# A new order table for a two-branch sequence kernel: positions, buffer slots and copy engines changed, the same operations

## The chip, the cores and the metric

One core of a Trainium2 chip. The metric is the device time of one launch in microseconds (us). Before the change three runs gave 343.4, 344.65 and 345.7 us, the median being 344.65.

## The reference, cut to what matters

Two independent branches over a sequence of 2048 positions with 1024 channels, all bf16; their outputs stand side by side in the last axis.

```python
# branch A: short convolution of k (4 taps), times v, long convolution by FFT, times q
kv = k_shift * v
y  = irfft(rfft(kv, 4096) * rfft(ssm_k, 4096))[:2048] + kv * ssm_D
a  = q * y
# branch B: diagonal complex recurrence between two dense complex products
Bu = einsum("bld,pd->blp", x, B_bar)
h  = Lam_bar * h + Bu[:, t]              # over t
b  = 2 * einsum("blp,dp->bld", hseq, Cmat).real + x * Dskip
```

## The kernel before, in words

Nothing in this kernel is scheduled by a tool at run time. The text table ORDER holds 1489 words, one for each task, and the loop at L773 to L783 takes them in turn and issues the instructions of each. Every engine runs its own instructions in the order in which they were issued; between engines only semaphores wait. So the table fixes the order on each engine, and only that. A word such as `ue.14.3:a2` has the task, its indices, and the slots it takes: `a` a unit of an SBUF area of 53 units (2 KB a partition each), `p` one of 8 PSUM banks, `h` one of 3 state buffers, `w` one of 3 slots for Fourier matrices. A task that takes a slot waits for the last reader of what lay there. A `v` behind the name of a copy (`uev`, `skev`, `a3ev` ...) puts that PSUM copy on DVE instead of ACT.

Branch B works in 16 chunks of 128 positions. On PE, `U.i.jp.jl` (L464, 16 matmuls of 128x128) is the input product; `ue` (L473) copies it out of PSUM. On DVE, `r1` (L487) and `r2` (L498) rotate, two `sc` (L504) are the scan, `r3` (L487) and `r4` (L510) rotate back, all 16 chunks one after the other; a one-column copy `cy.i` on ACT (L500) hands the state from `r4.i-1` to the scan `sc.i`. The output product is `y` (L520, L523) or, in quarters of the array, `yq` (L538, 20 matmuls a task); `ye` (L556) copies it out, and `yst`, `ysg` (from POOL's queue), `ysp`, `ysh` (from SP's) store it.

Branch A is an FFT in stages. DVE forms kv in `kvm`, `kva`, `kvb`, `kvc` (L588 to L603); PE does the first stage in `am` (L608) for kv and in `hT` (L632) and `hm` (L657) for the filter; `ae` (L614), `hc` (L637) and `he` (L665) copy out, and stores to DRAM regroup the rows. For 16 pairs of frequency groups `sh` and `sk` (L688) make the second stage, `she` (L697) and `ske` (L704) copy out, a DMA (`sw` on POOL's queue, `swp` on SP's, L708) swaps real and imaginary rows, `pr` on DVE (L714) multiplies, `sa` on PE (L726) goes back, `sae` (L734) copies, `vst` stores. The last stage loads with `vl`, multiplies in `a3` (L754), copies in `a3e` (L761), multiplies with q in `qm` (L763) and stores with `ost` or `osp`.

At the start ACT also copies out the transposed B matrices (`bc`, L431, 16 of them, of which DVE does two as `bcv`, L427 and L429) and makes the rotation tables: `sin1`, `sin2` (L325, L332), `eo` (L348, L349), `z1`, `z2` (L357 to L362); DVE finishes a table in `stt` (L354, L355).

The loop that issues everything, and the one dependency that it adds by hand:

```python
for word in ORDER.split():
    task, _, slots = word.partition(":")
    ...
    E[f](*args)
```

Of the kernel before, what the change touches and what calls it, by code (L numbers as in the profile page):

```python
# [72 lines left out]
bT.2.1:p0 U.0.0.1 bT.3.0:p7 bc.5.0 bc.2.1 bc.5.1 kva.3 kring U.1.2.0:p5 bl.3.1:a23 cl.0.0:a14 bT.2.0:p2 bT.3.1:p0
bl.7.1:a46 ue.1.0:a34 U.0.2.1:p6 bc.3.1 bc.2.0 U.0.2.0 U.1.2.1 cl.3.0:a37 bl.7.0:a26 cl.1.0:a25 bT.7.1:p2 kvb.3:a22
bT.7.0:p0 ue.0.0:a23 bc.6.1 kp.-2 x.3:a21 U.0.1.0:p3 bc.3.0 gz stt cl.2.0:a12 cT.0.0:p4 bc.7.0 bc.7.1 U.0.1.1 U.0.3.0:p0
kvm.1:a15 ue.1.2 vp.1:a27 U.0.3.1 U.3.2.0:p1 ue.0.1 U.3.0.0:p3 z1 kvm.2:a42 z2 ld_Q U.1.1.1:p2 ue.0.2 ue.0.3 x.2:a52
U.1.1.0 cl.3.1:a13 kva.1 cT.1.0:p7 cl.2.1:a32 kva.2 kvb.1:a14 kvb.2:a39 ue.1.1 kvm.0:a15 rta kvc.3 U.3.0.1 cx.6.0 kva.0
# [10 lines left out]
he.0.7.0.0:a50 y.0.0.3 hc.0.0:a13 hm.0.6.0:p4p2 ye.0.0:a19 hm.0.4.1:p5p7 y.0.1.0:p6 y.0.1.1 y.0.1.2 y.0.1.3 vp.2:a34
kvb.4:a31 he.0.6.0.0 sc.1.1 he.0.4.1.1 vp.3:a26 r1.2:a14 he.0.4.1.0 he.0.7.0.1 hst.0.7.0 r3.1:a46 hm.0.0.1:p1p5
hst.0.4.1 hc.0.5:a42 he.0.6.0.1 r4.1 hm.0.0.0:p2p3 he.0.0.1.0:a48 cy.2:h1 r2.2 hm.0.5.1:p7p0 ye.0.1 he.0.5.1.1:a23  # L90
he.0.5.1.0 kp.3 he.0.0.1.1 kvm.6:a38 he.0.0.0.0 y.1.1.0:p4 kvc.4 y.1.1.1 hst.0.6.0 hst.0.6.1 kp.4 kva.6 hst.0.5.1
hm.0.5.0:p6p0 he.0.5.0.0 kvm.5:a14 y.1.1.2 he.0.0.0.1 kvb.6:a25 he.0.5.0.1 y.1.1.3 hm.0.7.1:p2p7 ye.1.1:a28 he.0.7.1.0
kva.5 am.4.0:p1p6 y.1.0.0:p4 he.0.7.1.1 x.4:a32 hm.0.3.0:p2p3 ae.4.0.0:a29 hm.0.3.1:p5p0 hst.0.0.1 hst.0.0.0
he.0.3.1.0:a36 kvc.6 y.1.0.1 he.0.3.1.1 hst.0.5.0 kvb.5:a12 sc.2.1 ae.4.1.0 he.0.3.0.1 kvm.7:a13 y.1.0.2 am.4.1:p1p7
hl.3.0:a40 he.0.3.0.0 hm.0.1.0:p5p0 y.1.0.3 he.0.1.0.0:a38 am.6.1:p5p6 ae.4.1.1 U.4.3.1:p7 he.0.1.0.1 ae.6.0.1:a17
hl.2.1:a44 U.4.3.0 kvc.5 ae.6.1.1 am.6.0:p6p5 U.4.0.0:p2 ae.4.0.1 ue.4.3:a23 U.4.1.1:p3 ae.6.0.0 hm.0.2.0:p0p6 ae.6.1.0
ye.1.0 kva.7 hm.0.1.1:p5p7 sc.2.0 hm.0.2.1:p1p4 hst.0.7.1 hl.3.1 he.0.2.0.0:a34 U.4.1.0 he.0.1.1.0 hl.2.0 he.0.2.1.1
# [5 lines left out]
y.2.0.2 kvm.8:a48 r4.3 y.2.0.3 he.1.7.1.0 ae.7.0.1 hc.1.2:a31 y.2.1.3 ye.2.0:a47 hm.1.4.1:p4p6 ae.7.1.1 kva.8
hm.1.7.0:p3p5 ye.2.1 yq.3.0:p1p0 hst.0.1.1 he.1.7.0.1 he.1.7.0.0 hm.1.4.0:p7p2 yst.2 he.1.4.1.0:a29 kvm.9:a39 lw.3:w1
kvb.8:a38 he.1.4.0.1 vp.4:a12 yq.3.1 yq.3.2 he.1.4.1.1 he.1.4.0.0 hm.1.3.0:p5p6 he.1.3.0.1:a15 hm.1.3.1:p3p4 he.1.3.1.0
hst.1.7.0 he.1.3.1.1 yq.3.3 hm.1.2.1:p7p6 x.6:a37 he.1.2.1.0:a19 kva.9 he.1.2.1.1 he.1.3.0.0 kvc.8 x.5:a36 lw.1:w2
kvb.9:a35 kvm.10:a47 U.6.1.0:p3 U.6.1.1 am.8.1:p6p7 ast.7 hst.1.7.1 r1.4:a40 kva.10 ae.8.1.1:a44 hst.1.4.1 ae.8.0.1
r2.4:h0 am.8.0:p5p2 ae.8.0.0 ae.8.1.0 hst.1.4.0 ue.6.1:a38 yq.3.4 yq.3.5 hm.1.2.0:p5p7 he.1.2.0.0 x.7:a27 kp.7
hm.1.5.1:p2p6 he.1.5.1.1:a51 he.1.5.1.0 hst.1.5.1 yq.3.6 yq.3.7 ye.3.1:a24 hm.1.5.0:p6p4 kvm.11:a28 he.1.2.0.1 hst.1.2.0
hm.1.0.1:p3p5 cy.4 he.1.5.0.0 kp.6 kvb.10:a33 U.5.1.1:p2 U.5.1.0 sc.4.0 U.6.3.0:p7 kva.11 sc.4.1 hst.1.3.1 ye.3.0  # L110
ue.5.1:a40 he.1.0.1.0:a17 U.5.3.1:p2 hm.1.0.0:p3p1 kvc.9 ast.8 he.1.5.0.1 hst.1.5.0 kvb.11:a46 hm.1.6.0:p0p6 he.1.0.0.0
he.1.0.0.1 he.1.6.0.1:a47 U.5.3.0 hst.1.2.1 hst.1.3.0 U.6.3.1 he.1.6.0.0 U.6.0.1:p1 hm.1.1.0:p6p0 ue.5.3 ysp.3
hm.1.1.1:p2p3 he.1.0.1.1 hm.1.6.1:p5p4 he.1.1.0.0:a22 U.6.0.0 r3.4:a42 he.1.6.1.0 kvm.13:a12 he.1.1.1.1 U.5.2.0:p6
ue.6.0 U.5.2.1 he.1.6.1.1 hst.1.6.1 r4.4 he.1.1.1.0 hst.1.1.1 U.7.0.0:p3 he.1.1.0.1 vp.5:a50 U.5.0.0:p0 hst.1.0.1
hst.1.0.0 kvc.10 am.9.0:p2p4 kvc.11 kva.13 U.7.0.1 ae.9.1.0:a29 kvm.15:a49 ae.9.0.0 ue.7.0:a24 U.5.0.1 U.7.3.0:p4 ue.5.0
am.9.1:p1p0 vp.7:a34 ae.9.0.1 x.10:a26 kvb.13:a17 U.7.3.1 vp.6:a42 am.10.0:p3p1 kvm.14:a18 kvm.12:a13 kva.15 yq.4.0:p5p2
yq.4.1 yq.4.2 yq.4.3 ae.10.0.0:a44 ae.10.1.0 ue.7.3 ae.9.1.1 am.11.1:p3p0 ue.5.2 U.7.1.0:p1 kvc.13 ue.6.3 am.10.1:p4p6
# [725 lines left out]
```

## Time and profile before

| | us |
|---|---|
| span of the profiled execution | 343.2 |
| median of three runs | 344.65 |
| busy: PE, DVE, ACT, POOL | 329.5, 325.1, 273.5, 68.9 |
| TensorE clock granted, mean | 0.996 of full speed |
| DMA | 100.83 MB in 62592 packets |

The profile was taken of one execution; its span, from the first instruction to the last, is 343.2 us, and the only time around it is that of the runs: 343.4 us for the lowest, 344.65 us in the median. Three engines are busy nearly throughout: PE 96% of the span, DVE 95%, ACT 80%. The share of a matmul group in the busy time counts matmuls that wait inside PE's pipeline; the distance from one start to the next is what a matmul costs when PE is not held up. The chain that ended last runs mostly through PE.

### The profile page before, as it was taken

The page shows a single profiled execution, that of the slowest core. Times are in us where ns is not written, and L with a number is a line of the kernel's source. Part 1 is how long each engine was busy: PE and PEld are TensorE (multiplying, and loading weights), DVE is VectorE, ACT ScalarE, POOL GpSimd, SP SyncE. Part 2 cuts the span into 40 slices and gives each one's busy share as a digit, 9 for nine tenths or more (in the row PEclk, how much of TensorE's full clock was granted, in tenths as well). Part 3 has the DMA queues.
Part 4 walks back from the last instruction along what each step waited for, and adds up shares of the span by engine and source line. Part 5 has one row for each costly group of instructions (what it writes and reads, how often), then busy time and mean ns, then how long its engine had stood idle before and what let it go on. Part 6 is the DMA issues. An engine that isn't in the chain of part 4 may idle for free.

```text
span 343.2 us, 11813 instructions
## 1 busy us (share of the span) xinstructions
PE 329.5 (96%) x5086; PEld 230.2 (67%) x5105; DVE 325.1 (95%) x263; ACT 273.5 (80%) x519; POOL 68.9 (20%) x111
## 2 busy tenths in 40 slices
...
GB/s 177 352 351 208 315 281 283 155 318 365 368 269 198 264 263 295 233 261 343 313 353 282 270 339 212 369 272 311 280 314 276 216 326 378 327 335 284 375 346 274
DMA packets 62592, 100.83 MB, mean 294 GB/s; under 512 B 29422, under 2 KB 31614, under 8 KB 62540
## 3 DMA queue, kind: packets, MB, share of 16 engines
...
## 4 chain that ended last, share of the span: by engine, by line
PE 74%; ACT 15%; DMA 4%; issue 3%; DVE 3%; SPq 0%; POOL 0%; DVEq 0%; POOLq 0%
PE bank L464 25%; PE bank L538 19%; PE bank L520 10%; PE bank L754 4%; PE bank L688 4%; PE bank L726 4%; PE bank L608 2%; PE bank L657 2%; ACT BT L431 2%; ACT arena L614 2%; ACT arena L473 2%; ACT CT L439 2%; ACT arena L637 2%; DMA wslot<-a_c_W 1%; DMA arena<-arena 1%
## 5 line engine op out<-in xcount | busy, mean ns | idle before, releaser
L464 PEld LDWEIGHTS <-BT 128*128 128x128 bf16 x2048 | 117.8, 98 | 14.4 <-issue 9.9
L464 PE MATMUL bank<-arena,BT 128*128 128x128 bf16 x2048 | 125.4, 221 | 1.1 <-ACT BT L431 0.9
L538 PE MATMUL bank<-CT,gslot 64*64 64x512 bf16 x1408 | 86.6, 378 | 0.0
L504 DVE TENSOR_TENSOR_SCAN gslot<-rtab,gslot 128x1040 bf16<-128x1040 f32 x32 | 73.0, 2311 | 0.5
L538 PEld LDWEIGHTS <-gslot 64*64 64x64 bf16 x1408 | 36.9, 107 | 30.8 <-issue 1.9
L473 ACT CAST arena<-bank 128x512 bf16<-128x512 f32 x63 | 40.5, 660 | 13.8 <-PE bank L464 13.4
L614 ACT CAST arena<-bank 128x512 bf16<-128x512 f32 x64 | 37.2, 680 | 6.7 <-PE bank L608 4.0
L697 ACT CAST arena<-bank 128x512 bf16<-128x512 f32 x63 | 35.0, 617 | 5.9 <-issue 2.8
L520 PE MATMUL bank<-CT,gslot 128*128 128x512 bf16 x153 | 38.5, 380 | 0.3
L665 ACT CAST arena<-bank 128x512 bf16<-128x512 f32 x64 | 35.2, 631 | 3.1 <-PE bank L657 3.0
L714 DVE TENSOR_TENSOR arena<-arena 128x4096 bf16<-128x4096 bf16 x16 | 36.5, 2280 | 1.1 <-DMA arena<-arena 1.0
L487 DVE TENSOR_TENSOR arena<-gslot,Z 128x4096 bf16<-128x4096 bf16 x16 | 36.6, 2287 | 0.8 <-DVE gslot L504 0.2
L704 ACT CAST arena<-bank 128x512 bf16<-128x512 f32 x60 | 34.4, 621 | 3.2 <-PE bank L688 3.0
L734 ACT CAST arena<-bank 128x512 bf16<-128x512 f32 x60 | 32.4, 616 | 5.5 <-PE bank L726 5.3
L487 DVE TENSOR_TENSOR arena<-arena,Z 128x4096 bf16<-128x4096 bf16 x16 | 36.5, 2280 | 0.1
L556 ACT CAST arena<-bank 128x512 bf16<-128x512 f32 x31 | 18.1, 599 | 16.6 <-PE bank L538 8.7
L588 DVE TENSOR_TENSOR arena<-arena 128x4096 bf16<-128x4096 bf16 (+3 forms) x16 | 30.0, 1881 | 0.0
L668 POOL DMA_DIRECT2D Ys_h<-arena x32 | 23.2, 735 | 25.5 <-ACT arena L665 20.2
L617 POOL DMA_DIRECT2D Ys_kv<-arena x16 | 11.2, 726 | 83.5 <-ACT arena L614 81.1
L520 PEld LDWEIGHTS <-gslot 128*128 128x128 bf16 x160 | 14.1, 98 | 15.9 <-issue 2.3
L688 PE MATMUL bank<-arena,wslot 64*64 64x512 bf16 x256 | 21.5, 382 | 0.3 <-DMA wslot<-a_c_W 0.3
L737 POOL DMA_DIRECT2D Vs<-arena x16 | 11.7, 731 | 46.3 <-ACT arena L734 41.3
...
## 6 DMA issues: line engine op xcount, KB each, us to landing
Ys_kv<-arena POOLq DMA_DIRECT2D x16, 512.0 KB, 5.6
...
arena<-Ys_h SPq DMA_DIRECT2D x16, 512.0 KB, 5.0
arena<-Ys_kv SPq DMA_DIRECT2D x16, 512.0 KB, 5.6
Vs<-arena POOLq DMA_DIRECT2D x16, 512.0 KB, 5.6
arena<-Vs SPq DMA_DIRECT2D x16, 512.0 KB, 6.7
...
arena<-in_A_k_dram SPq DMA_DIRECT2D x8, 512.0 KB, 5.2
```

The costliest lines, as they stand in the source:

```text
L464: nc.tensor.matmul(pu[:, w, jl, :], BT[:, 2 * jp + jl, w, d, :], xT[:, d, :], start=(d == 0), stop=(d == ND - 1))
L473: cp(st["u", i][:, :, 2 * jp:2 * jp + 2, :], st.pop(("pu", i, jp)))
L487: nc.vector.tensor_mul(m, s_, win(Z))
L504: nc.vector.tensor_tensor_scan(gf, rtab[:].rearrange("p j t -> p (j t)"), gf, 0.0, ALU.mult, ALU.add)
L520: nc.tensor.matmul(py, h[:, w, j, 2:GW], CT[:, j, w, dh * 512:(dh + 1) * 512], start=(j == 0 and w == 0), stop=False)
L538: mm = nc.tensor.matmul(st["py", i, dh][cols, cs(r)], lhs(dh, rows, c), rhs(dh, rows), start=first, stop=last)
L614: cp(st["ysb", n2][:, p, dh * 512:(dh + 1) * 512], st.pop(("pa", n2, p, dh)))
L665: cp(o, st.pop(("pb", hf, s, e, r)).rearrange("p (n c t) -> p n c t", n=2, c=2))
L688: nc.tensor.matmul(st["ps", nm, g, l][64 * dh:64 * dh + 64, :], st["w", i][rows, a * WC:a * WC + 64], st[nm, i][rows, a, dh * 512:(dh + 1) ...
L697: cp(st["hab", i][:, 0, a, l, :], st.pop(("ps", "h", g, l)))
L704: cp(st["x16", i][:, a, l, :], st.pop(("ps", "k", g, l)))
L714: nc.vector.tensor_mul(hab, st.pop(("x16", i)).rearrange("p a l d -> p (a l d)").unsqueeze(1).to_broadcast([P, 2, 2 * D]), hab)
```

## The change

Only the table is new; every other line of the program is the same. It has 1489 words again, each task of before once. What differs:

- the position of most words, and the slots that they take;
- which engine copies out of PSUM: 22 copies on DVE before (2 of B matrices, 4 `skev`, 4 `saev`, 1 `shev`, 1 `uev`, 1 `yev`, 9 `a3ev`), 14 now (3 `uev`, 6 `yev`, 1 `skev`, 4 `a3ev`), so eight more are on ACT;
- which queue stores the output of branch B: three whole-chunk stores moved from SP (7 to 4) to POOL (7 to 10), and one half-chunk store from POOL to SP; the eight stores of branch A are 3 on SP and 5 on POOL where they were 4 and 4.

The core of the diff, the table's first and last rows:

```diff
 ORDER = """
-ld_w:a22 wb.3:p3 ld_par wbe.3:a8 par_T:p4 wb.0:p5 wb.7:p1 p32 ld_F bl.1.0:a39 bl.0.1:a18 wb.5:p7 bl.6.0:a34 bl.4.1:a14
-exp1 dve2 wbe.0 dve3 wb.6:p2 wb.4:p3 wb.2:p0 sm_pre wbe.7 bl.0.0:a27 wbe.5 x.0:a38 wb.1:p7 wbe.6 exp2 kp.1:a0 bl.1.1:a21
...
-y.15.1.3 ysg.14.1 ost.3 ye.15.1:a1 ysg.15.1 y.15.0.0:p4 y.15.0.1 a3e.15.0 y.15.0.2 qm.7 osp.7 y.15.0.3 ye.15.0 ysh.15.0
+ld_w:a13 ld_par par_T:p3 p32 bl.5.1:a27 dd bl.0.1:a17 bl.0.0:a39 exp1 kp.0:a0 wb.3:p2 dve2 bl.1.1:a40 bl.5.0:a42 kp.1
+wb.5:p4 wbe.3:a8 bl.1.0:a51 x.0:a52 dve3 tabA1:a44a28a35a37 sm_pre wb.4:p0 wb.7:p1 wbe.5 kp.-1 wbe.4 tabA2 wb.6:p6 wbe.7
...
+ysg.14.1 yev.15.0:a41 ost.0 ysh.15.0 ye.15.1 ysh.15.1
```

Three places show what this does to the engines.

DVE near the end of the frequency stage. L714 is `pr` (two of the rows are `pr.14` and `pr.13`), L487, L498, L504 and L510 are the steps of a chunk, and the number of a gslot tells the chunk's buffer. Before:

```order
L487 TENSOR_TENSOR arena_95<-gslot2_91,Z2_78 128x4096
L704 CAST arena_95<-bank6_102 128x512
L714 TENSOR_TENSOR arena_95<-arena_95 128x4096
L510 TENSOR_TENSOR gslot2_91<-arena_95 128x16x128
L714 TENSOR_TENSOR arena_95<-arena_95 128x4096
L734 CAST arena_95<-bank2_98 128x512
L487 TENSOR_TENSOR arena_95<-arena_95,Z1_77 128x4096
L498 TENSOR_TENSOR gslot0_89<-arena_95 128x16x128
```

Now:

```order
L487 TENSOR_TENSOR arena_95<-gslot2_91,Z2_78 128x4096
L510 TENSOR_TENSOR gslot2_91<-arena_95 128x16x128
L714 TENSOR_TENSOR arena_95<-arena_95 128x4096
L473 CAST arena_95<-bank5_101 128x2x256
L487 TENSOR_TENSOR arena_95<-arena_95,Z1_77 128x4096
L498 TENSOR_TENSOR gslot1_90<-arena_95 128x16x128
L704 CAST arena_95<-bank2_98 128x512
L714 TENSOR_TENSOR arena_95<-arena_95 128x4096 x2
```

The end of chunk 12 (L510) and the first two steps of chunk 13 (L487, L498) are now ahead of `pr.14`, which is the first of the two L714 in the last row (the L714 above it is `pr.12`); before, `pr.14` was the first L714 shown and all three stood behind it.

ACT around the hand-over of the state to chunk 3, `cy.3`, which is the L500 row in the middle. Before:

```order
L637 COPY arena_95<-bank5_101 128x1024
L637 COPY arena_95<-bank6_102 128x1024
L637 COPY arena_95<-bank4_100 128x1024
L614 CAST arena_95<-bank7_103 128x512
L500 COPY gslot2_91<-gslot1_90 128x16
L645 ACTIVATE arena_95<-arena_95,p32_118 128x1 x2
```

Now:

```order
L614 CAST arena_95<-bank4_100 128x512
L614 CAST arena_95<-bank1_97 128x512
L637 COPY arena_95<-bank7_103 128x1024
L473 CAST arena_95<-bank5_101 128x2x256
L500 COPY gslot0_89<-gslot1_90 128x16
L637 COPY arena_95<-bank3_99 128x1024
```

The copy just ahead of `cy.3` is now a `ue` (L473), which needs a `U` of PE; before it was an `ae` (L614).

ACT at the start, from `exp2` (L293) on. Before:

```order
L293 ACTIVATE r<-a__130 128x8
L314 ACT_TABLE_LOAD
L314 ACTIVATE so<-sv 128x16
L431 ACTIVATE BT<-bank_100 128x1024
L408 CAST arena<-bank_96 128x4x128
L408 CAST arena<-bank_103 128x4x128
L325 ACTIVATE arena<-arena,hpi 128x1024
L408 CAST arena<-bank_99 128x4x128
L431 ACTIVATE BT<-bank_102 128x1024
L332 ACTIVATE arena<-arena 128x1024
L431 ACTIVATE BT<-bank_97 128x1024
L348 ACTIVATE arena<-arena,b_224 128x128
```

Now, the rows just ahead of the same L348:

```order
L408 CAST arena<-bank_98 128x4x128
L314 ACT_TABLE_LOAD
L314 ACTIVATE so<-sv 128x16
L431 ACTIVATE BT<-bank_101 128x1024
L431 ACTIVATE BT<-bank_97 128x1024
L431 ACTIVATE BT<-bank_99 128x1024
L325 ACTIVATE arena<-arena,hpi 128x1024
L332 ACTIVATE arena<-arena 128x1024
L348 ACTIVATE arena<-arena,b_229 128x128
```

Six copies of B matrices (L431) are now ahead of the 16 instructions of `eo`, which begin with L348; before there were three.

More of the change, by code (lines that the diff above doesn't have):

```diff
@@ L73 @@
[L73 to L77, printed above, removed]
@@ L88 @@
[L88 to L92, printed above, removed]
@@ L93 @@
[L93 to L97, printed above, removed]
@@ L103 @@
[L103 to L107, printed above, removed]
@@ L108 @@
[L108 to L117, printed above, removed]
@@ new lines @@
+wbe.6 bT.0.1:p7 exp2 ld_Q bc.0.1 bT.5.1:p0 bc.5.1 bl.4.1:a41 wb.2:p2 wbe.2 bl.3.0:a27 bT.0.0:p7 bc.0.0 wb.0:p0 wb.1:p2
+wbe.0 wbe.1 kvm.3:a17 bT.5.0:p5 bT.1.0:p1 sin0 par_rest bT.1.1:p3 bc.5.0 ld_F bc.1.0 U.0.0.0:p2 x.1:a51 bl.6.1:a49
+bc.1.1 sin1 sin2 eo U.0.2.1:p3 U.0.0.1 ue.0.0:a47 kva.3 bT.6.1:p5 U.1.0.0:p6 bl.4.0:a39 bl.7.0:a30 bT.7.0:p1 bl.2.1:a16
+bc.7.0 bT.4.1:p4 bc.4.1 U.1.0.1 gz bT.4.0:p2 bc.4.0 bT.2.1:p1 kring kvm.1:a12 bl.7.1:a50 bc.2.1 bT.7.1:p4 bl.2.0:a22
+bc.7.1 bT.2.0:p0 bc.2.0 kvm.2:a23 kvb.3:a42 U.0.2.0 kp.-2 kva.2 kva.1 bl.6.0:a31 kvb.2:a39 lw.0:w0 bT.6.0:p7 bc.6.0
@@ new lines @@
+cl.2.0:a50 U.2.2.1:p2 U.2.2.0 ue.2.2 ast.2 cT.2.0:p7 cc.2.0 cT.2.1:p0 cc.2.1 sc.1.1 U.2.3.1 ue.2.3 hT.0.0:p2 hc.0.1:a31
+kva.4 hc.0.0:a19 hT.0.5:p5 hc.0.5:a26 hT.0.4:p7 hc.0.4:a32 y.0.0.0:p1 y.0.0.1 hT.0.7:p3 hc.0.7:a34 ld_G y.0.0.2
+hm.0.6.1:p6p2 he.0.6.1.1:a22 he.0.6.1.0 y.0.0.3 hst.0.6.1 hm.0.7.0:p5p4 he.0.7.0.0:a49 he.0.7.0.1 r3.1:a13 hst.0.7.0
+kvb.4:a24 hm.0.4.0:p3p7 he.0.4.0.1:a29 he.0.4.0.0 hm.0.4.1:p2p0 he.0.4.1.1 he.0.4.1.0 hst.0.4.1 cx.5.1 hst.0.4.0 r4.1
+kp.3 kvm.6:a41 ye.0.0:a17 cx.5.0 cx.7.0 cx.4.1 cx.7.1 cx.4.0 y.0.1.0:p6 y.0.1.1 y.0.1.2 hm.0.0.0:p3p7 he.0.0.0.0:a47
```

190 lines of the change are left out of this document (105 added, 85 removed).

## The prediction

> **What bounds the kernel now.** I read the busy times first, then the waits of DVE, then the chain that ended last, then the end of the program in the timeline.
>
> ```profile
> PE 329.5 (96%) x5086; PEld 230.2 (67%) x5105; DVE 325.1 (95%) x263; ACT 273.5 (80%) x519; POOL 68.9 (20%) x111
> PE 74%; ACT 15%; DMA 4%; issue 3%; DVE 3%; SPq 0%; POOL 0%; DVEq 0%; POOLq 0%
> ```
>
> Two engines look full, and the chain is PE's. The first row cannot tell which of the two is the bound; the waits say more.
>
> ```profile
> DVE p L284 <- PE bank L279: 3.5, 1, 3.5
> DVE arena L601 <- PE bank L415: 1.3, 1, 1.3
> DVE arena L714 <- DMA arena<-arena: 1.0, 2, 0.6
> ```
>
> DVE waits 3.5 us for the first parameters, and after that hardly ever: 1.3 us once at the start, 1.0 us in all for two swap DMAs, the rest less. So DVE runs on its own work from 4.48 us on. PE reads what DVE makes, and arrives just behind it:
>
> ```profile
> 279.11 2.28 DVE L714 TENSOR_TENSOR arena<-arena 128x4096 bf16<-128x4096 bf16 x1
> ...
> 281.31 1.49 PE L726 MATMUL bank<-arena,wslot 64*64 64x512 bf16 x24
> ...
> 222.09 2.28 DVE L714 TENSOR_TENSOR arena<-arena 128x4096 bf16<-128x4096 bf16 x1
> ...
> 224.43 1.06 PE L726 MATMUL bank<-arena,wslot 64*64 64x512 bf16 x16
> ```
>
> `pr.14` ends on DVE at 281.39 us. The three `sa` from 281.31 us are sa.24, sa.28 and sa.29; sa.28, the first reader of pr.14, is the second third of the row and starts about 0.4 us behind pr.14's end. `pr.6` ends at 224.37 us, and sa.12 starts 0.06 us later. Behind each such meeting PE has only its own work. So the time is **DVE's work up to a result, plus PE's work from that result's reader to the end, for the pair where this sum is largest**, plus waits and the tail:
>
> ```profile
> 336.05 1.03 PE L520 MATMUL bank<-CT,gslot 128*128 128x512 bf16 x4
> ...
> 336.97 1.03 PE L520 MATMUL bank<-CT,gslot 128*128 128x512 bf16 x4
> 337.83 0.22 PE L523 MATMUL bank<-Dd,arena 128*128 128x128 bf16 x1
> ...
> 335.52 1.23 DVE L763 TENSOR_TENSOR arena<-arena 128x2048 bf16<-128x2048 bf16 x1 [0.73 <-ACT arena L761]
> ...
> 302.11 1.07 ACT L556 CAST arena<-bank 128x512 bf16<-128x512 f32 x2 [4.63 <-PE bank L538]
> ...
> 338.70 0.34 SPq L560 DMA_DIRECT2D out_dram<-arena  x1
> ```
>
> PE ends at 338.05, 1.3 us after DVE's last instruction (336.75); a copy, a store of 128 KB issued at 338.70 and its landing fill the 5.15 us to 343.2.
>
> **The change, part by part.** What a task costs on PE is the distance between starts when PE runs on:
>
> ```profile
> 163.19 4.57 PE bank L464 x80
> 176.56 0.86 PE bank L726 x16
> 296.52 7.28 PE bank L538 x160
> 306.56 1.73 PE bank L754 x8
> ```
>
> A `U` (16 matmuls) is 0.90, an `sa` (8) 0.43, a `yq` (20) 0.90, an `a3` (2) 0.43, and a `y` 0.92 by the two L520 rows above. On DVE:
>
> ```profile
> 312.10 2.28 DVE L487 TENSOR_TENSOR arena<-arena,Z 128x4096 bf16<-128x4096 bf16 x1
> 314.30 1.28 DVE L761 CAST arena<-bank 128x512 bf16<-128x512 f32 x2
> 315.50 1.21 DVE L498 TENSOR_TENSOR gslot<-arena 128x2048 bf16<-128x2048 bf16 x1
> ...
> 308.44 1.22 DVE L510 TENSOR_TENSOR gslot<-arena 128x2048 bf16<-128x2048 bf16 x1
> 309.59 1.28 DVE L761 CAST arena<-bank 128x512 bf16<-128x512 f32 x2
> ```
>
> From start to start an `r1` is 2.20, a copy 0.60, an `r2` or `r4` 1.15.
>
> *The meeting of DVE and PE.* At pr.14 and sa.28, before: PE has 4 sa, 12 U, 16 yq, 32 a3 and 16 y left, 1.7 + 10.8 + 14.4 + 13.8 + 14.7 = 55.4 us, and from 281.77 that makes 337.2; it ends at 338.05, so 0.9 us are lost behind. Now DVE does one r1, one r2 and one r4 more ahead of pr.14 (+4.5) and six copies fewer (11 to 5, -3.6): +0.9. PE has three U fewer left and one sa more: -2.3. The sum at this pair falls by 1.4. I made the same count at every result of DVE that PE reads. Before, the largest sums lie together: pr.6 with sa.12, pr.14 with sa.28 (0.1 less) and r4.10 with yq.10.0 (0.2 less). At pr.6 DVE now has 2.3 less ahead (no r1.10 and no B copies, but r4.9: -2.20 - 1.20 + 1.15) and PE the same behind; at r4.10 DVE has 1.2 less (the two B copies, which are ACT's now) and PE the same. So r4.10 and pr.14 carry the end now, and the largest sum falls by **1.4 us**, not by all the eight copies. Bounds: 0, if a pair that I rate lower takes over through a wait of its own, and -2.3, by the pair that falls most.
>
> *The eight copies.* On DVE they were 8 x 0.60 = 4.8 us. Most of them leave behind the last meeting (nine `a3ev` become four), where PE no longer waits for DVE. On ACT they are free there: the L556 row above stands behind an ACT gap of 4.63 us, and ACT is busy 17.3 of the last 43 us.
>
> *The start.* The 1.3 us that DVE waited for PE at L601 (kvb.3, whose slot was that of a B matrix still being transposed) goes; kvb.3 takes other units and stands two kvm later. In its place r1.0 comes to wait for ue.0.1 on ACT:
>
> ```profile
> 27.76 3.81 ACT L431 ACTIVATE BT<-bank 128x1024 bf16<-128x1024 bf16 x4
> 31.38 1.15 ACT L473 CAST arena<-bank 128x512 bf16<-128x512 f32 x2
> 32.32 1.16 ACT L357 ACTIVATE Z<-Z 128x1024 bf16<-128x1024 bf16 x1
> ```
>
> A B copy is 0.90 from start to start, a 512-column copy 0.48. Ahead of ue.0.1 ACT has 16 B copies (14.4), 8 wbe and 5 ue (6.2), eo (4.7) and 3.5 of exp, sin and z1: 28.8, from 4.8 us with a table load of 1.3, so ue.0.1 ends near 35.6. DVE has 30.3 of work ahead of r1.0 and is there near 35.2: a wait of 0.4 for one of 1.3. Bounds 0 and -1.3; I take **-0.9**.
>
> *ACT in the first 100 us.* Here a wait is added.
>
> ```profile
> 14.73 0.44 ACT L348 ACTIVATE arena<-arena,b 128x128 f32<-128x128 f32 x1
> ...
> 19.41 1.92 ACT L431 ACTIVATE BT<-bank 128x1024 bf16<-128x1024 bf16 x2
> ...
> 35.16 1.13 ACT L362 ACTIVATE Z<-arena 128x1024 bf16<-128x1024 f32 x1
> ...
> 49.12 2.28 DVE L487 TENSOR_TENSOR arena<-gslot,Z 128x4096 bf16<-128x4096 bf16 x1
> ...
> 94.69 0.38 ACT L500 COPY gslot<-gslot 128x16 bf16<-128x16 bf16 x1
> ...
> 95.19 4.53 DVE L504 TENSOR_TENSOR_SCAN gslot<-rtab,gslot 128x1040 bf16<-128x1040 f32 x2
> ...
> 0.00:100.00 100.00, 93.15 (x1151) 73.21 (x1161) 92.93 (x111) 93.94 (x162) 22.63 (x41) 1.00 0.99 288
> ```
>
> The L500 row is cy.3; the scan behind it started 0.12 us after it ended, so it had no slack. Ahead of cy.3 ACT now has two B copies, one ue, one ae and two short adds more, 2 x 0.90 + 2 x 0.48 + 0.4 = 3.1 or 3.2 us; DVE has 1.0 more ahead of that scan. If ACT were always busy, DVE would wait 2.1 us. But ACT was busy 93.9 of the first 100 us, and the first 4 were its start, so some 2 us of pauses can take it up. Bounds 0 and +2.1; nearer to the lower, I take **+0.7**. Behind a late scan are r3.3 and every later step of DVE, and so PE.
>
> *Stores and loads.* Three stores of 256 KB go from SP's queue to POOL's. POOL is busy 20%, and its stores land as soon as SP's transfers (5.6 us for 512 KB on each):
>
> ```profile
> Ys_kv<-arena POOLq DMA_DIRECT2D x16, 512.0 KB, 5.6
> ...
> arena<-Ys_kv SPq DMA_DIRECT2D x16, 512.0 KB, 5.6
> ```
>
> Nothing of it is on the path: 0. The tail keeps its form, copy and 128 KB store on SP: 0; a 512 KB store on POOL's queue just ahead of it could add up to 1.
>
> The sum: -1.4 - 0.9 + 0.7 = **-1.6 us**, from a span of 343.2 to 341.6. The runs' median stands 1.45 above that span, so 344.65 becomes **343.0**.
>
> **The rivals.** *DVE is the bound.* If PE's place behind DVE were only an accident of the old order, all of DVE's saving would be time: 4.8 + 0.9, less the 0.7 at cy.3 = 5.0, 344.65 to **339.6**. For it: 95% busy and hardly a wait. Against it: DVE's last instruction ends 1.3 us ahead of PE's, and PE's last 55 us hold 0.9 us of waits. The Trainium skill, Perfetto Trace Analysis, section Identifying the Most-Contended Engine, has this rule: matmul busy time overstates how full PE is, and LDWEIGHTS busy should be used, with the engine of highest occupancy improved first. By that PE's 67% would leave DVE's 95% as the engine to relieve; the trace agrees that busy PE time is inflated (a matmul of L464 is shown for 221 ns and costs 0.90 us / 16 = 56), but PE's starts follow each other without a gap at the end, which goes against the rule here.
>
> ```profile
> L464 PE MATMUL bank<-arena,BT 128*128 128x128 bf16 x2048 | 125.4, 221 | 1.1 <-ACT BT L431 0.9
> ```
>
> *ACT becomes the bound of the first 100 us: slower.* `eo` (14.73 to 19.41 us before) starts behind six B copies instead of three, some 3 us later, and with it the ACT tasks that DVE waits for (z2, the last ue of chunks 3 and 1, cy.3). In the old order z2 ended at 36.29 and its reader r3.0 started at 49.12, 12.8 us later; now r3.0 has 3.4 us less of DVE's work ahead of it and z2 8.4 us more of ACT's, which leaves 1 us. Once ACT pauses for PE in that stretch by over 1 us in all, each further microsecond goes to DVE. Pauses as before, 2 to 3 us, with eo's 3.1 and cy.3's 2.1 give +5.2; with -1.4 and -0.9 that is +2.9: **347.5**. For it: 93.9 of 100 us busy, and more work there. Against it: ACT's pauses were waits for PE, and PE's order is now ahead of ACT's in this stretch, so they should shrink.
>
> *Slots at the last moment.* `x.1` on SP's queue now takes the slot of a B matrix and waits for its transpose (bT.1.0); eight B loads behind it on that queue wait too. Ahead of that transpose PE has 5.3 us of work, from 4.2 us on, and waits for some copies of ACT: x.1 goes out near 11.3 us, where it went out at 7.82:
>
> ```profile
> 7.82 1.74 SPq L447 DMA_TRANSPOSE arena<-in_B_x_dram  x1
> ```
>
> If its 3.5 us are not hidden behind ACT's eo, the U of chunk 1 and the last B copies come late and take back the 1.4 us: the old time, **344.6**.
>
> **How the numbers follow.** Forecast 0.50, DVE the bound 0.26, ACT the bound 0.17, late slots 0.07. A measurement here tells about 1% from no change, 3.4 us: faster is below 341.2, slower above 348.1. The forecast's own range is 340.7 to 345 by its bounds; a tenth of it lies below 341.2. Faster: 0.05 + most of the 0.26 = 0.29. Slower: under half of ACT's 0.17, which reaches 350, and a little for what I do not see: 0.13. Within 1%: 0.58. The range goes from 339.0, the middle of the DVE case and a little more, to 347.5.
>
> **What would show it.** Right: DVE's last instruction ends several us ahead of PE's; sa.28 still starts within 1 us of pr.14's end; no L601 wait at the start; PE's end near 336.5 with the same 5 us behind it. The ACT rival shows as DVE waiting on L500, L473 or L360 to L362 for 2 us or more before 100 us. The DVE rival shows as PE ending at 333 to 334. Wrong at the root would be a DVE wait of over 2 us on a DMA after 150 us.

## The result: slower by 1.4%, and the profile after

The changed kernel takes 349.16 us (median of six runs, 347.23 to 351.38) where the kernel before takes 345.42 (six runs). The two medians lie 3.7 us apart. The ratio on record is 1.0136, with a 95% interval of 1.0104 to 1.0169, which on 345 us is 4.7 us; below, this ratio is used, since every experiment has one like it. The forecast was 343.0, 1.6 us less than before. The profiled execution took 349.38, its span is 347.6. Two executions of the experiments, 354.65 and 360.73 us, ran slower at a granted clock of 0.986 and 0.978; the ratios leave them out, and the second of them is the one that was profiled for the reverse by slots.

First the busy times and DVE's waits after the change, to be held against the two shown of before:

```profile
PE 330.8 (95%) x5105; PEld 230.5 (66%) x5105; DVE 322.4 (93%) x255; ACT 277.8 (80%) x527; POOL 70.7 (20%) x114
...
DVE arena L763 <- ACT arena L761: 3.3, 3, 1.9
DVE p L284 <- PE bank L279: 3.1, 1, 3.1
DVE arena L714 <- ACT arena L704: 2.9, 3, 1.6
DVE gslot L504 <- ACT gslot L500: 2.6, 1, 2.6
DVE arena L487 <- ACT arena L473: 2.0, 3, 0.9
```

DVE has less work, as the change says, and yet arrives later. Before, its waits on ACT were one of 0.7 us and one of 0.4; now ten of the fifteen waits that the list of after has, 10.8 of their 16.2 us, are for ACT. Where that counts, the windows of DVE show: first of before, up to pr.14 and from there to the end, then of after, cut at the same place (columns: the stretch, its length and DVE's busy time, then granted clock, DMA share and GB/s).

```profile
4.50:279.10 274.60, 269.04 (x221) 1.00 0.97 289
279.10:343.20 64.10, 55.91 (x41) 0.98 0.93 331
```

```profile
4.50:285.80 281.30, 271.60 (x217) 1.00 0.94 287
```

pr.14 comes 6.7 us later: 2.6 us more of busy time and 4.1 more of waits (5.6 before, 9.7 now). Half of the additional busy time lies in one place, the eight instructions of `dd`, which the new table puts first and which take 1.25 us longer there, one row of after and one of before:

```profile
4.45 2.63 DVE L371 TENSOR_SCALAR Dd<-ident,p 128x128 bf16<-128x128 bf16 x8
```

```profile
11.84 1.38 DVE L371 TENSOR_SCALAR Dd<-ident,p 128x128 bf16<-128x128 bf16 x8
```

The delay builds up along the way: r1.0 starts 1.8 us earlier than before, sc.3.0 2.0 us later, pr.3 2.8 us later and pr.14 6.7. From pr.14 to the end it is 64.1 us before and 347.6 - 285.8 = 61.8 now, 2.3 less. The meeting itself still stands, in the timeline of after:

```profile
285.83 4.48 DVE L714 TENSOR_TENSOR arena<-arena 128x4096 bf16<-128x4096 bf16 x2
...
288.38 1.49 PE L726 MATMUL bank<-arena,wslot 64*64 64x512 bf16 x24
```

pr.14, the first of the two, ends at about 288.1, and sa.28 starts 0.3 us later. So the meeting held, and the whole loss lies ahead of pr.14.

ACT's waits show something that the kernel before has not. Of before, no row of ACT's waits names a DMA. Of after, three do:

```profile
ACT arena L614 <- DMA Ys_kv<-arena: 2.8, 2, 2.0
...
ACT arena L665 <- DMA Ys_h<-arena: 1.5, 1, 1.5
ACT arena L704 <- DMA Vs<-arena: 1.3, 1, 1.3
```

These are stores to DRAM. At three places ACT's copy waits until the store that still reads its slot has landed: ae.1.0.0 for ast.3 (1.96 us), he.0.3.0.1 for hst.0.6.0 (1.54) and ske.17.0 for vst.5 (1.35). Such a wait is called a hold from here on. The three are 4.8 us in all, of which 3.9 lie after the end of the copy's own matmul, so that no more than these are the store's alone. The rows add up to 5.6, which is the number in the expectations below, but the second wait of the first row, 0.83 us in front of ae.13.1.1, is no hold. By the table that copy writes units 28 and 29, while ast.11, the store that lands just then, reads 23 and 24; and the copy's own matmul, the last of the second row here, ended 0.04 us before the copy began:

```profile
147.43 0.58 ACT L614 CAST arena<-bank 128x512 bf16<-128x512 f32 x1 [0.83 <-DMA Ys_kv<-arena]
```

```profile
146.79 0.59 PE L608 MATMUL bank<-arena,F1t 128*128 128x512 bf16 x2
```

In the profile of the kernel with two places mended by order (below) the same 0.83 us stand in front of that copy, although ast.11 had landed 1.8 us earlier. So the table fixes more than the order on each engine: its slots decide which copy has to wait for which store. The timeline at the first of the three, ae.1.0.0:

```profile
47.69 0.84 ACT L614 CAST arena<-bank 128x512 bf16<-128x512 f32 x1
...
50.48 0.58 ACT L614 CAST arena<-bank 128x512 bf16<-128x512 f32 x1 [1.96 <-DMA Ys_kv<-arena]
50.96 0.59 ACT L473 CAST arena<-bank 128x512 bf16<-128x512 f32 x1
51.44 1.10 ACT L614 CAST arena<-bank 128x512 bf16<-128x512 f32 x2
51.61 0.59 PE L608 MATMUL bank<-arena,F1t 128*128 128x512 bf16 x2 [1.73 <-ACT arena L473]
```

ACT stands still from about 48.5 to 50.48. The copy behind it, ue.1.3 (L473), needed nothing of that store, but ACT runs in order; and am.2.0 on PE needs the bank that ue.1.3 empties, so PE stands too. Why the store was still there, the list of DMA issues from 40.5 to 41.5 us says (last column: us from issue to landing):

```profile
arena<-in_A_ssm_k_dram SPq DMA_DIRECT2D x1, 512.0 KB, 10.1
Ys_kv<-arena POOLq DMA_DIRECT2D x1, 512.0 KB, 9.7
arena<-in_A_k_dram SPq DMA_DIRECT2D x1, 512.0 KB, 10.8
```

ast.3 was issued with two loads of its size and took 9.7 us, where the stores of this kind took 5.6 in the median before and at most 7.05 (4.8 in the median in this execution). The Trainium skill, DMA: Bandwidth & Descriptors, section Anatomy of one DMA — SWDGE (gpsimd) path, fits one DMA of POOL as 2.0 us plus its bytes over 436 KB per us; an estimate from that is 3.2 us for 512 KB. The 9.7 measured here is three times that. The two loads issued beside it took 10.1 and 10.8; that sharing the DMA engines with them is what made the store slow was not tested.

### The profile page after: what moved, and what is told of

The parts are those of the page before. It is cut to its first block, busy times and chain, and to the rows that moved or that the text cites. A ratio compares the mean times of both kernels' runs of the same rounds, so it can differ in the third digit from the quotient of the medians.

```text
span 347.6 us, 11826 instructions
## 1 busy us (share of the span) xinstructions
PE 330.8 (95%) x5105; PEld 230.5 (66%) x5105; DVE 322.4 (93%) x255; ACT 277.8 (80%) x527; POOL 70.7 (20%) x114
## 5 line engine op out<-in xcount | busy, mean ns | idle before, releaser
L504 DVE TENSOR_TENSOR_SCAN gslot<-rtab,gslot 128x1040 bf16<-128x1040 f32 x32 | 72.7, 2310 | 3.2 <-ACT gslot L500 2.6
L473 ACT CAST arena<-bank 128x512 bf16<-128x512 f32 x61 | 38.8, 653 | 14.2 <-PE bank L464 13.9
L614 ACT CAST arena<-bank 128x512 bf16<-128x512 f32 x64 | 36.0, 643 | 7.3 <-PE bank L608 4.5
L714 DVE TENSOR_TENSOR arena<-arena 128x4096 bf16<-128x4096 bf16 x16 | 36.3, 2284 | 2.9 <-ACT arena L704 2.9
L487 DVE TENSOR_TENSOR arena<-arena,Z 128x4096 bf16<-128x4096 bf16 x16 | 36.6, 2286 | 2.2 <-ACT arena L473 2.0
L487 DVE TENSOR_TENSOR arena<-gslot,Z 128x4096 bf16<-128x4096 bf16 x16 | 36.6, 2288 | 0.3
L617 POOL DMA_DIRECT2D Ys_kv<-arena x16 | 11.0, 724 | 84.7 <-ACT arena L614 84.7
## 6 DMA issues: line engine op xcount, KB each, us to landing
arena<-in_A_k_dram SPq DMA_DIRECT2D x8, 512.0 KB, 10.8
```

The lines of the kernel that those rows point to most:

```text
L473: cp(st["u", i][:, :, 2 * jp:2 * jp + 2, :], st.pop(("pu", i, jp)))
L487: nc.vector.tensor_mul(m, s_, win(Z))
L504: nc.vector.tensor_tensor_scan(gf, rtab[:].rearrange("p j t -> p (j t)"), gf, 0.0, ALU.mult, ALU.add)
L614: cp(st["ysb", n2][:, p, dh * 512:(dh + 1) * 512], st.pop(("pa", n2, p, dh)))
L714: nc.vector.tensor_mul(hab, st.pop(("x16", i)).rearrange("p a l d -> p (a l d)").unsqueeze(1).to_broadcast([P, 2, 2 * D]), hab)
```

## Experiments

All of them are edits of the order table. Each edited kernel was measured beside the kernel before on the same chip. Ratios are to the kernel before, with 95% intervals; the changed kernel's is 1.0136 (1.0104 to 1.0169), from its six runs alone, and it was not measured again beside its edits. Each profile is of one execution, so a difference of single waits between two profiles is a hint and no more.

### Hand-overs of ACT to DVE

**cy.3 ahead.** The longest of DVE's waits is that for cy.3.

```diff
 hl.3.1 hdv.3
+r4.2
 hT.1.6:p0 hT.1.2:p1 hc.1.2:a17
+cy.3
 hT.1.7:p2 hc.1.7:a36
...
 hT.1.1:p7 hc.1.1:a52
-r4.2
 kvm.8:a46 U.4.0.1 ue.4.0
-cy.3
 sc.3.0 hc.1.3:a15
```

> The changed kernel with cy.3 taken ahead of nine copies on ACT (r4.2 and cy.3 issued right behind hc.1.2), nothing else. Theory A (the sum of the prediction holds, but DVE's waits for ACT ahead of pr.14 were sized wrong): the 2.67 us wait of sc.3.0 goes and all later results of DVE come earlier by as much, 349.2 - 2.6 = 346.6. Rival B (PE's own waits for banks, which rose by 4.8 us, are the loss, and DVE's waits hide behind them): no change, 349.2. Rival C (the eight copies more on ACT are too much work for it, wherever they stand): no change, 349.2, and the wait turns up again at the next hand-over.

Measured: 348.86 (347.29 to 350.85, nine runs), ratio 1.0121 (1.0085 to 1.0156). In the timeline of DVE (this kernel's table has two rows more, so every line number is two higher: L506 is the scan, L716 pr, L706 ske):

```profile
96.34 2.32 DVE L506 TENSOR_TENSOR_SCAN gslot<-rtab,gslot 128x1040 bf16<-128x1040 f32 x1
```

```profile
173.64 2.29 DVE L716 TENSOR_TENSOR arena<-arena 128x4096 bf16<-128x4096 bf16 x1 [1.52 <-ACT arena L706]
175.95 2.29 DVE L489 TENSOR_TENSOR arena<-gslot,Z 128x4096 bf16<-128x4096 bf16 x1
180.28 2.29 DVE L716 TENSOR_TENSOR arena<-arena 128x4096 bf16<-128x4096 bf16 x1 [2.04 <-ACT arena L706]
```

The scan starts 3.1 us earlier and waits for nothing. But pr.3 starts at 180.28, within 0.01 us of where it started in the changed kernel (180.29): the gain is given back in front of pr.1 and pr.3. Theory A is wrong here.

**Three copies in the frequency stage, and both edits.**

```diff
 yq.5.3 sw.0.0
+ske.6.1 ske.6.0
 ske.1.1:a13 sk.0:p7p5 ske.1.0
-ske.6.1
 sa.2:p6p1
-ske.6.0
...
 sk.17:p6p3 sk.13:p7p4
+ske.13.0 ske.13.1
 ske.17.0:a19
...
-ske.13.0
...
-ske.13.1
...
-she.31.0
 sk.21:p1p4 ske.21.0 ske.20.0
+ske.21.1 she.31.0
 she.31.1
-ske.21.1
```

> The changed kernel with three copies to DVE's products put ahead on ACT in the frequency stage: ske.6.1 and ske.6.0 ahead of ske.1.1, ske.13.0 and ske.13.1 ahead of ske.17.0, and she.31.0 and she.31.1 behind ske.21.1. Theory A: the waits of pr.3 (0.78), pr.6 (1.71) and pr.10 (0.68) go, 349.2 - 3.2 = 346.0; 347.5 if one of them only moves to the next product. Rival B: pr.6's wait goes, but sk.16 still waits 1.58 us for its bank, 349. Rival C: 349.

> Both of these together. Theory A: 2.6 + 3.2 = 5.8 less, 343.4, about the time of the prediction, with sa.28 still starting within 1 us of pr.14's end. Rival B: 349 or, with PE's waits in another place, 348. Rival C: 349, since ACT has the same work.

Measured: 348.83, ratio 1.0118 (1.0069 to 1.0166), and 350.84, ratio 1.0155 (1.0101 to 1.021). Again nothing clear of the changed kernel's interval. With both edits DVE waits at other hand-overs: for cy.7 and cy.12 (the scans, L506) and for ue.13.2 (r1.13, L489; the numbers are two higher again).

```profile
DVE arena L489 <- ACT arena L475: 3.1, 3, 2.0
DVE gslot L506 <- ACT gslot L502: 2.3, 2, 1.5
DVE arena L716 <- ACT arena L706: 1.7, 2, 1.5
```

**The reverse in the kernel before**, cy.3 made late:

```diff
 ae.5.0.1:a15 yst.1
-cy.3
 y.2.1.0:p7 kp.5
...
 hc.1.7:a30 ae.5.1.1
+cy.3
 hst.0.2.1 hT.1.2:p4
```

> The kernel before with one word moved: cy.3 on ACT behind six more instructions (hd.2, ae.5.1.0, ae.5.0.0, hc.1.7, ae.5.1.1 and what PE makes them wait), where it ends some 2.4 us later than the scan of chunk 3 wants it. Theory A: 2.4 us of DVE's time ahead of every later meeting, 345.4 + 2.4 = 347.8. Rival B: no bank of PE is held longer, 345.4 to 346. Rival C: ACT's work is the same, 345.4.

Measured: 347.36 against 344.54, ratio 1.0069 (1.0044 to 1.0094), 2.4 us, what theory A expected. So in the order before a late hand-over is time, and in the new order its removal is not: there something else comes late as well. One such place is on PE: sk.6, whose copy pr.3 needs, starts at 175.1 us in the changed kernel and at 173.3 in the kernel before.

### Stores that still read a slot

Theory D takes the three stores of ACT's waits. Two were mended by order, that is, the copies were moved, and one by a slot:

```diff
 am.1.0:p4p7
-ae.1.0.0
 U.1.3.0 ue.1.3 r1.1:a12 ae.1.1.0
+ae.1.0.0
 ae.1.0.1
...
-he.0.3.0.1
 kvb.5:a34
-he.0.3.0.0
...
 ae.4.1.0 ae.4.0.1
+he.0.3.0.1 he.0.3.0.0
 y.1.0.2
```

> The changed kernel with two copies on ACT that waited for a store to leave their slot put behind copies that were ready: ae.1.0.0 behind ue.1.3 and ae.1.1.0, and he.0.3.0.1 with he.0.3.0.0 behind ae.4.1.1, ae.4.1.0 and ae.4.0.1. Theory D (ACT is held by slots that a store to DRAM still reads; PE then waits for the banks behind, and the hand-over cy.3 is late because ACT is): PE's waits at am.2.0 (1.90), hm.0.2.0 (0.82) and U.4.3.0 (0.55) shrink to about 0.6 in all, sc.3.0 waits under 1 us instead of 2.67, and PE and DVE come to the frequency stage 2.5 us earlier together: 346.6. Theory E (both stand at 175 us before the loads of that stage, whatever came ahead): not more than the 1 us that the profile with cy.3 moved showed, 348.2. Theory A in its first form (only DVE's waits count): the gain is what goes from sc.3.0, under 0.5 by what moving cy.3 gave.

```diff
 sk.17:p6p3 sk.13:p7p4
-ske.17.0:a19
+ske.17.0:a11
 ske.17.1
```

> The changed kernel with one slot changed: ske.17.0 takes unit 11, free since 208.5 us, in place of unit 19, whose store vst.5 landed at 219.89. Theory D: ACT's 1.4 us at ske.17.0 go, with them sk.16's 1.58 on PE and pr.6's 1.71 on DVE, 349.2 - 1.5 = 347.7. Theory E: the same, since this lies behind the loads. Rival C (too much work for ACT): pr.6 waits as before, 349.2.

> Both together, three places where a copy on ACT no longer waits for a store. Theory D: 2.6 + 1.5 = 4.1 less, 345.1, the time of the kernel before. Theory E: 1.0 + 1.5 less, 346.7. Rival C: 349.

> The same with cy.3 ahead on ACT as well (behind hc.1.2). Theory D: the rest of sc.3.0's wait goes too; what stays is the later start of PE (1.4 us) and the waits of pr.3, pr.10 and r1.13: 344.6. Theory E: no more than the one without it, 346.7, because DVE then stands in front of pr.1 and pr.3 as it did when cy.3 alone was moved.

Measured: the two by order 347.12, ratio 1.0087 (1.0053 to 1.0122); the slot 348.94, 1.0118 (1.0091 to 1.0145); all three 346.57, 1.0079 (1.0054 to 1.0105), whose interval just touches the changed kernel's; all three with cy.3 ahead 348.26, 1.0118 (1.0083 to 1.0153). So the two by order give something back, with intervals that still overlap the changed kernel's, and the one by slot alone nothing that is clear of it; its place, ske.17.0, was held in the changed kernel's profile, but not in those with cy.3 ahead, with the three copies and with the two by order, which all have that slot unchanged. The moves of the two by order also bring other copies forward (ue.1.3 among them), and no run separates that from the hold. In the profile of the two by order, DVE's wait for cy.3 is 1.0 us instead of 2.6, without cy.3 being touched:

```profile
DVE gslot L504 <- ACT gslot L500: 1.0, 1, 1.0
```

That would fit if part of this late hand-over was ACT's hold. But in the kernel with the slot alone, whose table is the changed kernel's up to 208 us, the wait was 1.2 us: the hold in front of he.0.3 did not occur in that execution, and DVE itself came later. So how much of the 2.6 is the hold is not shown.

For cy.3 ahead taking the gain away again there is a row that fits, though it covers half of the 1.7 us at most. ACT and PE of the last kernel:

```profile
94.63 0.28 ACT L500 COPY gslot<-gslot 128x16 bf16<-128x16 bf16 x1 [1.03 <-DVE gslot L510]
95.00 1.01 ACT L637 COPY arena<-bank 128x1024 bf16<-128x1024 bf16 x1
95.90 0.59 ACT L473 CAST arena<-bank 128x512 bf16<-128x512 f32 x1
```

```profile
96.55 0.67 PE L632 MATMUL bank<-ident,arena 128*128 128x128 bf16 x8 [0.90 <-ACT arena L473]
```

Put there, cy.3 makes ACT wait 1.03 us for DVE, the copies behind it come late, and hT.1.1 on PE waits 0.90. Here DVE's wait was exchanged for one of PE.

### The loads of the frequency stage

The loads lk wait for the last of the stores ast. In the changed kernel ast.13 had all its copies at 150.0 us but stood behind ast.12 in POOL's queue, and three stores left together at 159.59. POOL's timeline of the changed kernel (L617 is ast):

```profile
154.61 0.69 POOL L617 DMA_DIRECT2D Ys_kv<-arena  x1 [10.26 <-ACT arena L614]
159.59 2.12 POOL L617 DMA_DIRECT2D Ys_kv<-arena  x3 [4.30 <-ACT arena L614]
```

The second row holds ast.12, ast.13 and ast.14. The edit:

```diff
 ae.15.1.1 am.14.0:p2p7
+ast.13
 ast.15
...
+ast.14
 ast.12
...
-ast.13
...
-ast.14
```

> The changed kernel with two stores ahead in POOL's queue: ast.13 (ready at 150.0 us, issued at 160.15 because it stood behind ast.12) ahead of ast.15, and ast.14 ahead of ast.12. Theory F (three chains end together at pr.1 and pr.3, near 175 to 180 us: DVE with its wait for cy.3, ACT and PE with their waits for stores, and the loads of the frequency stage, which wait for the last of these stores): the loads lk come 2 us earlier, but DVE is no earlier at pr.1, so only pr.3's wait of 0.78 goes, 348.4. Rival G (16 DMA engines are 88 to 100% busy from 161 to 181 us, so that only the sum of the bytes counts): lk.0 lands at 177.7 us as before and nothing changes, 349.2.

> The same with cy.3 ahead on ACT, which by itself gave 348.86. Theory F: two of the three chains are earlier by 2 to 2.6 us; PE's is the last, 0.7 us earlier, so sk.6 starts near 174.4 and pr.3 near 179: 347.8. If PE has more slack there than I think, 346.6. Rival G: lk.0 lands at 177.7 and pr.3 starts at 180.3 again, 348.9.

> The stores ahead, with the three places where a copy on ACT no longer waits for a store (346.57 without the stores ahead, its profile with pr.3 waiting 0.97 for what lk.0 brings). Theory F: 346.57 - 0.9 = 345.6. Rival G: 346.6.

> All of it. Theory F: DVE, PE and the loads all come 2 us or more earlier to 175 us; what stays against the kernel before is PE's later start, 1.4 us, against the 2.3 us less that lie behind sa.28: 344.8, at or under the kernel before, and 3.5 us under the same without the stores ahead (348.26). Rival G: 348, as without.

Measured, in this order: 348.98, ratio 1.0145 (1.0105 to 1.0185); 348.17, 1.0115 (1.0089 to 1.0141); 347.18, 1.0081 (1.0052 to 1.0111); 349.40, 1.0138 (1.0108 to 1.0167). Rival G has the mechanism wrong: in the changed kernel with nothing but cy.3 moved, lk.0 landed at 177.7 us, and with the stores ahead as well at 172.7. But its times, no gain, are the ones that came, and theory F is wrong where it expected a gain. With the loads 5 us earlier, DVE of the second kernel still waits for ACT at pr.1 and pr.3:

```profile
173.31 2.29 DVE L714 TENSOR_TENSOR arena<-arena 128x4096 bf16<-128x4096 bf16 x1 [1.50 <-ACT arena L704]
175.52 2.29 DVE L487 TENSOR_TENSOR arena<-gslot,Z 128x4096 bf16<-128x4096 bf16 x1
178.88 2.29 DVE L714 TENSOR_TENSOR arena<-arena 128x4096 bf16<-128x4096 bf16 x1 [1.07 <-ACT arena L704]
```

and other stores held ACT. The third kernel, with three places mended, has these rows:

```profile
ACT arena L614 <- DMA Ys_h<-arena: 2.7, 1, 2.7
ACT arena L473 <- DMA Ys_kv<-arena: 1.8, 2, 1.0
ACT arena L473 <- DMA out_dram<-arena: 1.2, 1, 1.2
ACT arena L614 <- DMA Ys_kv<-arena: 0.7, 1, 0.7
```

The slots of hst.1.1.1 (2.7), ast.10 and ast.7, which held nothing in the changed kernel's profile, hold ACT here, and 0.7 us at ae.1.0.0 are left; the third row is the copy ue.15.0, whose matmul ended 0.04 us before it and whose slot no store reads. That makes 5.1 us of holds, about as much as the changed kernel's 4.8, and yet the profiled execution took 347.43 where that one took 349.38: the sum of the holds alone does not give the time.

Why other places hold can be counted from the two traces and the tables. Of ACT's copies that write where a store has read, 6 of 73 start within 1 us of that store's landing in the changed kernel, and 1 of 60 in the kernel before; within 3 us it is 15 and 6. So the new table has more slots whose store is only just gone.

### A fourth slot, the start, and the reverse

Four kernels: a slot more for ae.10 (on top of the three places mended, so two places by order and two by slot; "four slots" below); the slots of two early loads exchanged, so that x.1 on SP's queue waits for an earlier transpose; both; and in the kernel before three slots changed so that a store still reads them.

```diff
 hst.1.5.0 am.10.1:p1p0
-ae.10.0.1:a35
+ae.10.0.1:a26
```

```diff
-bl.0.0:a39
+bl.0.0:a51
...
-bl.1.0:a51
+bl.1.0:a39
```

```diff
-ye.3.1:a24
+ye.3.1:a52
...
-ske.5.0:a13
+ske.5.0:a50
...
-ske.17.1:a16
+ske.17.1:a34
```

> The changed kernel with four places mended where a copy on ACT waits for a store that still reads its slot: the three of the earlier run (346.57) and ae.10.0.1 on unit 26, free since 131 us, in place of 35, whose store hst.1.1.1 held ae.10.1.0 by 0 to 2.8 us, other in each execution. Theory D (slots of stores): 345.8, and a narrower spread than 347 to 351. Rival H (PE alone sets the first 175 us, from its later start on, and ACT's holds matter no more): 346.6 as with three.

> The changed kernel with the slots of bl.0.0 and bl.1.0 exchanged, so that x.1 on SP's queue waits for the transpose bT.0.0 (from 8.8 us) and not for bT.1.0 (13.5 us), and the loads behind it leave 2 to 3 us earlier. The waits of bT.7.0 (1.62) and part of those beside it go. Theory H: PE is the bound from its start to 175 us, so 349.2 - 1.5 = 347.7. Theory D: PE's later waits for banks take it up, DVE's wait for cy.3 stays, 348.9.

> Both. If both causes add, 345.8 - 1.5 = 344.3, the time of the kernel before. If only the slots count, 345.8; if only the start, 347.7.

> The kernel before with three slots changed and nothing else: ye.3.1 takes unit 52, ske.5.0 unit 50 and ske.17.1 unit 34, where a store landed 2.8, 2.9 and 2.1 us after the copy's start in the profile of before. So ACT is held three times, 7.8 us at most, as the changed kernel's three held it for 5.6. Theory D: each hold goes on to PE's banks and DVE's products at about half its length, 344.4 + 3 = 347.5. Rival (ACT is idle for 20% of the span and makes it up): 344.5.

Measured: four slots 346.35 (344.88 to 348.90, twelve runs), ratio 1.0058 (1.0033 to 1.0084), clear of the changed kernel's interval; the start alone 348.51, 1.0129 (1.01 to 1.0159); both 346.25, 1.0053 (1.0028 to 1.0079). The runs of the four-slot kernel spread over 4.0 us, those of the changed one over 4.2; that part of theory D failed. The four mends together give back 2.7 of the 4.7 us; what the fourth adds to the three is not clear of the noise (1.0058 beside 1.0079). ACT's waits for stores in the four-slot profile are one row, of which 0.76 us are a hold, at ae.1.0.0 still; the other 0.88 are the wait of ae.13.1.1 for its matmul:

```profile
ACT arena L614 <- DMA Ys_kv<-arena: 1.6, 2, 0.9
```

With the start alone, x.1 left at 11.95 us where it left at 14.57, and bT.7.0 waits no more; but a wait for a copy of ACT stands at bT.4.0, the row below, and PE was hardly earlier behind it (U.1.2.1 at 28.6 where it was at 28.7). So the edit moved the wait, and what an earlier start would be worth stays untried.

```profile
23.66 0.61 PE L415 MATMUL bank<-ident,arena 128*128 128x128 bf16 x8 [0.72 <-ACT arena L473]
```

The reverse: five runs with a median of 352.06 (348.88 to 353.65), ratio 1.0218 (1.0174 to 1.0263), 7.5 us, where theory D expected 3 and its rival nothing. Its profile has a span of 359.0 us, so only the holds are read from it:

```profile
ACT arena L556 <- DMA Ys_h<-arena: 3.3, 1, 3.3
ACT arena L704 <- DMA out_dram<-arena: 2.8, 1, 2.8
ACT arena L704 <- DMA Vs<-arena: 2.3, 1, 2.3
```

Three words of 1489 differ from the kernel before, in the slot alone. They cost 7.5 us though ACT is idle for 20% of the span before, and they hold ACT for 8.4 us in the profiled execution. How much of a hold is time can't be had from these two numbers, since they are not of the same executions; but theory D, which took half of a hold as time, was 2.5 times too low. This is the cleanest evidence for the holds: the order is the same, and nothing but the slots differs.

### The copies alone, and all that was mended

In the kernel before, three copies go from DVE to ACT at their places. In the changed one with the four slots, three hand-overs of ACT go ahead as in the second experiment (without ske.13), and cy.7.

```diff
-skev.27.0
+ske.27.0
...
-saev.28.1:a16
+sae.28.1:a16
...
-a3ev.10.0
+a3e.10.0
```

```diff
 pr.3
+r4.6
 sae.2.0
+cy.7
 sa.7:p3p1
...
-r4.6
-cy.7
 yq.6.0:p7p3 pr.0
```

> The kernel before with three of its copies on ACT instead of DVE, at the same places of the table: skev.27.0, saev.28.1 and a3ev.10.0. By the sum of the forecast only the first lies ahead of a meeting that PE waits for (pr.14), and pr.6 with sa.12 keeps the end: 344.3, no change. If DVE is the bound (the first rival), 344.5 - 3 x 0.6 = 342.7. If ACT is too late at these places, 345.5.

> The changed kernel with the four slots mended, and three hand-overs of ACT to DVE put ahead: ske.6.0 and ske.6.1 ahead of ske.1.1, cy.7 (with r4.6) ahead of sae.7.0, ske.21.1 ahead of she.31.0 and she.31.1. If the waits of pr.3 (1.2) and pr.10 (0.6) are time once the holds are gone: 346.3 - 1.5 = 344.8, the time of the kernel before. If they only move to the next product, as they did with the holds in place: 346.3.

Measured: 344.37 against 344.26, ratio 0.9989 (0.9965 to 1.0014), and 347.54, ratio 1.0105 (1.0063 to 1.0147). The copies are worth nothing by themselves, as the sum said. The Trainium skill, Perfetto Trace Analysis, section Identifying the Most-Contended Engine, would improve the engine of highest occupancy first, DVE by its measure; moving the three copies took 1.4 us off DVE's busy time (325.1 to 323.7; 1.8 was the estimate) and changed nothing that could be measured, so the rule did not hold here. In the mended kernel pr.3 starts at 177.2, even ahead of the kernel before (177.5), but pr.14 at 283.1 where the kernel before has 279.1. Most of that difference is work: between the two DVE is busy 2.9 us longer than in the kernel before and waits 1.4 longer. Of the waits for ACT there, at pr.6, sc.12 and r1.13, only the one at sc.12 is new against the changed kernel. Up to pr.14:

```profile
DVE gslot L504 <- ACT gslot L500: 2.4, 2, 1.6
DVE arena L487 <- ACT arena L473: 1.3, 2, 0.7
DVE arena L714 <- ACT arena L704: 1.2, 1, 1.2
```

None of the eighteen kernels is measurably faster than the kernel before.

## Why the prediction was wrong, step by step

**The form of the sum held.** sa.28 starts within 1 us of pr.14's end, as named. What lies behind pr.14 fell by 2.3 us, which is the number counted for U and sa, but partly by luck: from sa.28 to the end of PE it is 1.6 us less, the tail behind PE's end, taken as unchanged, is 0.6 less, and the meeting itself 0.1. That copies on DVE are free agrees with the three moved alone, two of them behind the meeting and one ahead of it, which give 0.9989.

**What lies ahead of pr.14 failed.** The prediction had +0.9 of work, -0.9 for the start and +0.7 for ACT, +0.7 in all. It became +6.7: 2.6 of work and 4.1 of waits. The range was mis-added as well: by the bounds that the prediction gives, -2.3 - 1.3 for the lower end and +2.1 (+1 more for the tail) for the upper, it runs from 341.0 to 346.8 or 347.8, not from 340.7 to 345. Even so it would not have held 349.16.

**The step that failed is "Stores and loads: nothing of it is on the path: 0".** I priced the stores by queue and by time to landing, and did not ask who takes the slot next. The prediction's rival "slots at the last moment" had the kind of thing but one place, x.1, and the edit of that place changed nothing that could be measured. What the runs show in its place: stores hold ACT for 4.8 us at three places of the changed kernel's profile and nowhere in that of before; four such places mended, two by order and two by slot, give back 1.0136 - 1.0058, 2.7 of the 4.7 us; and three slots put into the kernel before cost it 7.5. So the stores were on the path, with a price in place of the 0. The remaining 2.0 us have no cause that a run shows. The sign that I gave for "wrong at the root", DVE waiting on a DMA, looked at the wrong engine: ACT waits for the DMA, DVE and PE wait for ACT.

**ACT in the first 100 us** was taken as +0.7 with an upper bound of 2.1; DVE waited 2.6 for cy.3. The bound counted work and not holds; with two holds mended the wait was 1.0, within the bounds, but with those holds left in the table another execution had 1.2, so that the holds made the difference is likely and not shown. And as time the wait was not worth its size: taken away whole, it left the ratio at 1.0121, with sk.6 on PE and the copies for pr.1 and pr.3 late as well.

**The start.** The wait at L601 went as foretold. In its place came one of 0.8 at the same line for another bank (kvb.4, L601 <- L632), not counted. The load x.1 left at 14.57 us, where the prediction had 11.3.

**DVE's work up to pr.14** was to rise by 0.9; its busy time rose by 2.6. Of the 1.7 us that were not counted, 1.25 are `dd`, put first, whose eight instructions took 2.63 us where they took 1.38.

**The rivals.** DVE as the bound is refuted by its own sign (PE ends at 343.1, not 333) and by the three copies alone. ACT as the bound of the first 100 us was nearest in time, 347.5, and its sign showed (DVE waiting over 2 us on L500 before 100 us); but its mechanism, too much work on ACT, is not the one that the runs bear out: with every copy left on its engine, the four mends give 2.7 of the 4.7 us back.

**What stays open.** 0.58%, 2.0 us, after the four mends; 1.7 us of it may be the work of DVE that was not counted, and no run tests this. Nor do the holds of a profile order the times: with 0.26 us of holds left, two profiled executions took 345.75 (two mended by order) and 349.05 (three mended), and in both pr.14 came still 3.0 to 3.2 us later than before. Of DVE's waits for single copies of ACT, those for cy.3, cy.7, ske.6 and ske.21 were edited, and each time another stood in their place or PE got one; cy.12 and ue.13 were not. No one cause for this rest was found; that the new order has ACT, DVE and PE meet with almost nothing to spare at many places is what the traces look like, but this was argued and not shown. Why the kernel with all mended hand-overs (1.0105) is not better than the one with the four slots alone (1.0058) is open as well, beyond the longer work of DVE up to pr.14; their intervals overlap a little.
